# A stored order in place of a list scheduler for the pieces of a banded-attention and MLP kernel

## The chip, the core and the metric

The kernel runs on one core of one Trainium2 chip. The metric is the device time of one launch in microseconds (us); the median of three runs of the kernel before is 668.6 us (666.87 to 668.98).

## The reference

Inputs are q, k, v with batch 4, 8 heads, 768 positions and head size 64, and an MLP with matrices of 512 x 2048 and 2048 x 512. What is computed:

```python
scores = scale * np.matmul(q, k.transpose(0, 1, 3, 2))
is_sink = pos[None, :] < int(n_sink)          # n_sink = 4
rel = pos[:, None] - pos[None, :]
in_window = (rel >= 0) & (rel < int(window))  # window = 128
scores = np.where(is_sink | in_window, scores, -1000000000.0)
a = np.exp(scores - np.max(scores, axis=-1, keepdims=True))
a = a / (np.sum(a, axis=-1, keepdims=True) + 1e-09)
attn = np.matmul(a, v)
x = attn.transpose(0, 2, 1, 3).reshape(B * S, H * D)   # 3072 x 512
h = x @ w_in
out = (h - np.tanh(h)) @ w_out
```

Everything is fp32, and the output is 3072 x 512.

## The kernel before, in words

**Tiling.** The function `_banded` cuts the 3072 tokens into 12 chunks of 256 (a batch and a third of its positions). Each chunk has four attention units u, a pair of heads each, so u runs from 0 to 47. The MLP is done chunk by chunk over 8 groups g of the hidden width, 96 steps n = (chunk, g).

**An attention unit.** Keys come by a DMA at L361, queries by two at L105 (the first twelve units; later L370), into a tile `qk`, `kraw` or `qraw`. Two score pieces on PE (L532 for the first twelve units, L539 after) make `s` and `o`: four matmuls each. DVE merges them with the masks (L554, L556), ACT takes the exponent (L564), DVE the sums and reciprocals (L584, L585), ACT scales (L590; POOL does it for every fourth of the first units, L594), POOL places the sink weights (L601). Then `turn` transposes the probabilities on PE (L624), ACT copies the whole (L631) and DVE two masked parts (L638). For two pairs at a time `attend` multiplies: the sink rows (PE L665, copied by ACT L672 to `zr`), the values (PE L681, L687, with v from the DMAs of L405), and the high and low words of the result (ACT L704, DVE L708) into `xall`, the MLP's input. The sinks' own values come by a DMA at L460, are made high and low words by ACT L466 and POOL L471, and are totalled by DVE L475.

**The MLP.** The raw weights come in halves by SP's queue (L416), DVE decodes them in three passes (L157, L159, L161), ACT and DVE make high and low words (L747, L751), and SP writes what is needed again to DRAM (L755, L761, L762, L765), from where it comes back through a ring of seven slots (L808). The first products (L823) are pieces of six matmuls; then tanh on ACT (L854), the difference on DVE (L857), high and low words (L860 and others; for the chunks from 5 on L873 and, low, L876 into `glbuf`). The second products are L905, or L939, where seven products of blocks stand for eight. Output goes out by POOL and, at the end, by SP and ACT (L996, L1020).

**What sets the order.** Every piece of work is put into a list with `Work.add`: its engine (a DMA counts with the engine that issues it), how long it takes, a due time, a function that issues its instructions, and what it reads and writes. There are 3002 pieces: PE 1038, ACT 593, DVE 748, POOL 194, SP 429. `Work.order` is a list scheduler: it goes through time, gives the engine that can start first the piece that can start on it, the one with the earliest due time first, and reckons delays from engine to engine (`WAKE`) and a time for a DMA to land. At the end of `_banded` the pieces are issued in the order that it gives. Every engine does its pieces in that order and waits, with all that stand behind, until what the next one needs is done.

**Decode buffers.** `turn` puts the transposed probabilities into one of four places m. The places 2 and 3 are also the buffers in which the weights are decoded (`wm[key] = pts[:, 2 + r]`, read and written under the name `("dw", r)`).

Of the kernel before, what the change touches and what calls it, by code (L numbers as in the profile page):

```python
# [169 lines left out]
class Work:  # L170

    WAKE = {"PE": 250, "ACT": 170, "DVE": 90, "POOL": 100, "SP": 80}

    def __init__(self, slack, pad, late, land):
        self.all, self.wrote, self.read = [], {}, {}
        self.slack, self.pad, self.late, self.land = slack, pad, late, land  # L180

    def add(self, engine, took, due, fn, reads=(), writes=(), lands=0, port=False):
        n = len(self.all)
# [9 lines left out]
        self.all.append((engine, took, due, fn, after - {n}, lands, port))  # L193

    def order(self):
        todo = {}
        for n, (engine, *_) in enumerate(self.all):
            todo.setdefault(engine, []).append(n)
        users, left = [[] for _ in self.all], [len(t[4]) for t in self.all]
        for n, t in enumerate(self.all):  # L200
            for a in t[4]:
                users[a].append(n)
        ready = {n: 0.0 for n, k in enumerate(left) if k == 0}
        waiting = {e: [n for n in v if n in ready] for e, v in todo.items()}
        free, port, start, done = dict.fromkeys(todo, 0.0), {}, {}, {}

        def at(n, e):
            t = max(free[e], ready[n])
            return max(t, port.get("DVE" if e == "POOL" else "POOL", 0.0)) if self.all[n][6] else t

        while any(waiting.values()):
            t, e = min((min(at(n, e) for n in v), e) for e, v in waiting.items() if v)
            n = min((n for n in waiting[e] if at(n, e) <= t), key=lambda n: (self.all[n][2], n))
            _, took, _, _, _, lands, locks = self.all[n]
            took *= self.pad if e in ("ACT", "DVE", "POOL") and self.all[n][2] > self.late else 1.0
            waiting[e].remove(n)
            start[n], free[e], done[n] = t, t + took, t + took
            if lands:
                free[e], done[n] = t + (took if e == "POOL" else lands), t + lands + (1700 if self.all[n][2] < self.late else self.land)
            if locks:  # L220
                port[e] = t + took
            for u in users[n]:
                f = self.all[u][0]
                lag = 0 if f == e else self.WAKE[e]
                if f == "PE":
                    lag += self.slack if self.all[u][2] > self.late else 100
                ready[u] = max(ready.get(u, 0.0), done[n] + lag)
                left[u] -= 1
                if not left[u]:
                    waiting[f].append(u)  # L230
# [1169 lines left out]
```

## Time and profile before

| | |
|---|---|
| median of three runs | 668.6 us (666.87 to 668.98) |
| the profiled execution, its own time | 670.4 us |
| its span in the profile | 668.6 us |
| PE (matmul) busy | 650.5 us, 97% |
| weight loads on PE | 603.3 us, 90% |
| DVE busy | 543.8 us, 81% |
| ACT busy | 396.9 us, 59% |
| POOL busy | 164.2 us, 25% |

The span is the time from the first to the last recorded instruction; 1.8 us of the profiled execution lie outside of it. PE is TensorE's matmuls, DVE is VectorE, ACT ScalarE, POOL GpSimd and SP SyncE, which here issues most of the DMAs. L532 is line 532 of the kernel before. In a line of a timeline stand the start and the length in us, the engine, the line, the operation, its output and inputs, and how many instructions the line stands for; in square brackets, how long the engine was idle before it and what ended that.

### The profile page before, as it was taken

Reading aid. Unit: us, or ns where it says so; the run is one execution under the profiler, and the core shown is the slowest. Engines: PE = TensorE matmul, PEld = TensorE weight load, DVE = VectorE, ACT = ScalarE, POOL = GpSimd, SP = SyncE. Lnnn points to the kernel's source line nnn. Section 1 sums busy time; section 2 is a strip of 40 time slices with the busy share of each in tenths; the row PEclk is TensorE's granted clock in tenths of the full one; section 3 lists DMA queues with packets and bytes.
Section 4 is the critical chain, followed back from the end, with each engine's and each line's share of the span. In section 5 each row is a group of like instructions: output and inputs, shape, how many; then the busy total and the mean of one; then the engine's idle time right before and its main releaser. Section 6 shows DMA issues by size and latency. Waiting matters only on the chain.

```text
span 668.6 us, 14547 instructions
## 1 busy us (share of the span) xinstructions
PE 650.5 (97%) x5099; PEld 603.3 (90%) x5099; DVE 543.8 (81%) x1399; ACT 396.9 (59%) x1024; POOL 164.2 (25%) x331
## 2 busy tenths in 40 slices
PE   6989999999999999999999999999999999999996
PEld 4668899999979899898999999999999999999995
DVE  6889999964999878578798899887899899855654
ACT  5987444345898667567665575676566566523321
POOL 5453100000873232243331212312213212100100
PEclk9899999999999999999999999999999999999999
DMA  5877788884999667899977767767776867656771
GB/s 172 279 254 273 260 268 308 292 289 143 226 212 279 217 205 226 236 291 279 287 221 219 223 208 239 251 185 209 243 221 203 266 182 209 206 165 210 259 199 40
DMA packets 79502, 152.97 MB, mean 229 GB/s; under 512 B 9596, under 2 KB 25852, under 8 KB 79420
## 3 DMA queue, kind: packets, MB, share of 16 engines
q1 hardware_dynamic: 65900, 121.52, 58.3%
q0 software_dynamic: 13376, 30.30, 16.1%
q8 instruction: 42, 0.69, 0.4%
q14 instruction: 40, 0.33, 0.1%
q10 hardware_dynamic: 144, 0.13, 0.1%
HBM read 131.47 MB, written 20.45 MB: 227 GB/s over the span
## 4 chain that ended last, share of the span: by engine, by line
PE 76%; DVE 8%; ACT 6%; DMA 4%; issue 2%; POOL 2%; SPq 0%; POOLq 0%; DVEq 0%; ACTq 0%
PE h L823 33%; PE s L939 10%; PE o L939 7%; PE o L905 6%; PE x L687 3%; PE s L905 3%; PE t L624 2%; PE t L687 2%; DMA kraw<-kp 2%; PE t L539 2%; PE t L905 2%; PE x L905 2%; PE x L539 1%; ACT p L590 1%; DVE pt L638 1%
## 5 line engine op out<-in xcount | busy, mean ns | idle before, releaser
L823 PE MATMUL h<-xall,ring 128*128 128x256 f32 x990 | 130.3, 279 | 0.0
L823 PEld LDWEIGHTS h<-xall,ring 128*128 128x128 f32 x990 | 121.1, 188 | 1.4 <-issue 0.7
L854 ACT ACTIVATE gbuf<-h 128x512 f32<-128x512 f32 x96 | 57.1, 595 | 91.4 <-PE h L823 67.6
L823 PE MATMUL h<-xall,spare 128*128 128x256 f32 x738 | 97.6, 279 | 0.0
L873 ACT CAST ghbuf<-gbuf 128x896 fp32r<-128x896 f32 x55 | 51.7, 940 | 68.5 <-DVE gbuf L870 68.4
L823 PEld LDWEIGHTS h<-xall,spare 128*128 128x128 f32 x738 | 90.9, 188 | 0.5
L370 POOL DMA_DIRECT2D qraw<-qd x36 | 26.6, 740 | 255.8 <-DVE q L511 199.9
L876 DVE TENSOR_TENSOR glbuf<-gbuf,ghbuf 128x896 fp32r<-128x896 f32 x55 | 60.0, 1090 | 20.4 <-ACT ghbuf L873 17.5
L564 ACT ACTIVATE p<-p,st 128x132 f32<-128x132 f32 x132 | 52.4, 399 | 12.9 <-DVE st L556 12.0
L857 DVE TENSOR_TENSOR gbuf<-h,gbuf 128x512 f32<-128x512 f32 x55 | 37.9, 689 | 22.9 <-ACT gbuf L854 22.4
L905 PE MATMUL o<-w,ghbuf 128*128 128x512 f32 x192 | 49.9, 395 | 0.2 <-ACT ghbuf L860 0.2
L823 PEld LDWEIGHTS h<-xall,w 128*128 128x128 f32 x384 | 46.9, 188 | 2.0 <-DVE w L751 0.4
L823 PE MATMUL h<-xall,w 128*128 128x256 f32 x384 | 48.2, 279 | 0.2 <-DVE w L751 0.2
L502 DVE TENSOR_TENSOR ks<-kraw,ks 64x392 fp32r<-64x392 f32 x72 | 40.4, 561 | 5.9 <-ACT ks L497 3.8
L590 ACT ACTIVATE p<-p,st 128x132 f32<-128x132 f32 x132 | 42.6, 395 | 3.1 <-DVE st L585 2.6
L905 PEld LDWEIGHTS o<-w,ghbuf 128*128 128x128 f32 x192 | 33.8, 188 | 6.1 <-ACT ghbuf L860 0.5
L857 DVE TENSOR_TENSOR h<-h,gbuf 128x512 f32<-128x512 f32 x41 | 28.5, 696 | 13.0 <-ACT gbuf L854 12.7
L497 ACT CAST ks<-kraw 64x392 fp32r<-64x392 f32 x72 | 37.1, 515 | 2.2 <-DMA kraw<-kp 1.3
L860 ACT CAST ghbuf<-h 128x512 fp32r<-128x512 f32 x41 | 24.0, 585 | 21.1 <-DVE h L857 20.4
L939 PE MATMUL s<-edge,ghbuf 128*128 128x256 f32 x220 | 35.3, 279 | 0.0
L939 PE MATMUL o<-w,ghbuf 128*128 128x256 f32 x220 | 35.1, 278 | 0.0
L939 PE MATMUL s<-w,ghbuf 128*128 128x256 f32 x220 | 35.1, 278 | 0.0
(185 smaller groups left out, 1546.5 us busy)
## 6 DMA issues: line engine op xcount, KB each, us to landing
ring<-wscr SPq DMA_DIRECT2D x165, 256.0 KB, 4.8
spare<-wscr SPq DMA_DIRECT2D x123, 256.0 KB, 4.7
qraw<-qd POOLq DMA_DIRECT2D x36, 256.0 KB, 5.2
...
```

Of the source, the lines that this page charges most:

```text
L497: nc.scalar.copy(ks[u][r, h, :], kt[u][r, :])
L502: (nc.gpsimd if KP else nc.vector).tensor_tensor(k[o, h, :], t[r, :], k[r, h, :].bitcast(F32), op=ALU.subtract)
L564: nc.scalar.activation(e, e, AF.Exp, bias=st[u][:, j : j + 1], scale=-1.0, accum_out=st[u][:, 4 + j : 5 + j],)
L590: nc.scalar.activation(pr[u][:, j, :], pr[u][:, j, :], AF.Copy, scale=s[:, 8 + j : 9 + j])
L687: nc.tensor.matmul(xps[key][(p - p0) // 2][h * 64 : h * 64 + 64, p % 2, a:z], lhsT=vt[cc, i][:, hd : hd + D], rhs=rhs, start=False, stop=p ...
L823: nc.tensor.matmul(hps[n][:, f, :], lhsT=w, rhs=x, start=r == 0, stop=r == 11)
L854: nc.scalar.activation(g0, h(), AF.Tanh)
L857: nc.vector.tensor_tensor(g0 if strassen(n) else h(), h(), g0, op=ALU.subtract)
L873: nc.scalar.copy(ghbuf[:, n % 2], gbuf[:, 1:, :])
L876: nc.vector.tensor_tensor(low7(n), gbuf[:, 1:, :], ghbuf[:, n % 2].bitcast(F32), op=ALU.subtract)
L905: nc.tensor.matmul(sums_of(n, cc, t), lhsT=a[:, f, t * P : (t + 1) * P], rhs=wt[1, g][:, (0, 1, 0)[i], f, :], start=first and not low and ...
L939: nc.tensor.matmul(acc, lhsT=a[:, b, :], rhs=factor(g, m, part % 2), start=g == 0 and part == 0 and m in (4, 1, 2, 7), stop=closes(n) and ...
```

## The change

The scheduler's loop is taken out, and `Work.order` unpacks a table: a permutation of the 3002 pieces, held as text. It asserts that each piece stands behind those that it depends on. The delays, allowances and the due times' use go with the scheduler. `turn` also names the decode buffers among what its copies for the places 2 and 3 read. The offset of the low words in `glbuf` is 4 for the steps 81, 84, 87, 90 and 93, where it was 4 or 44 for 81, 83, 86, 89 and 92.

```diff
-    WAKE = {"PE": 250, "ACT": 170, "DVE": 90, "POOL": 100, "SP": 80}
-
-    def __init__(self, slack, pad, late, land):
+    ORDER = (
+        "c-jruV*?mA69C}k?vhI`wQbwBZQHhO+qP|Et8KemyVb^4uJ8LBo==ZfN{v;ZCMctv3JO&uMJlQqr{=5iDu$Y<teT{}TBH^zR+H62"
...
+    )
+
+    def __init__(self):
         self.all, self.wrote, self.read = [], {}, {}
-        self.slack, self.pad, self.late, self.land = slack, pad, late, land
...
     def order(self):
-        todo = {}
...
-        while any(waiting.values()):
-            t, e = min((min(at(n, e) for n in v), e) for e, v in waiting.items() if v)
-            n = min((n for n in waiting[e] if at(n, e) <= t), key=lambda n: (self.all[n][2], n))
...
-        return sorted(start, key=lambda n: (start[n], n)), start
+        from base64 import b85decode
+        from struct import iter_unpack
+        from zlib import decompress
+
+        todo = [n for n, in iter_unpack("<H", decompress(b85decode(self.ORDER)))]
+        at = {n: i for i, n in enumerate(todo)}
+        assert len(at) == len(todo) == len(self.all)
+        assert all(at[a] < at[n] for n in todo for a in self.all[n][4])
+        return todo
...
-        work = Work(SLK, PAD, LATE, LAND)
+        work = Work()
...
-        ASIDE = {81: 4, 83: 44, 86: 4, 89: 44, 92: 4}
+        ASIDE = {n: 4 for n in (81, 84, 87, 90, 93)}
...
             if c == 0:
-                work.add("ACT", 260, d + 1400, whole, ["t"], [("pt whole", m)])
-            work.add("DVE", 430 if c == 0 else 710, d + 1500, lambda: part(1, below), ["t"], [("pt own", m)])
+                work.add("ACT", 260, d + 1400, whole, ["t"], [("pt whole", m)] + [("dw", m - 2)] * (m > 1))
+            free = [("dw", m - 2)] * (m > 1)
+            work.add("DVE", 430 if c == 0 else 710, d + 1500, lambda: part(1, below), ["t"], [("pt own", m)] + free)
...
-                work.add("DVE", 430 if c == 0 else 710, d + 1500, lambda: part(0, after), ["t"], [("pt before", m)])
+                work.add("DVE", 430 if c == 0 else 710, d + 1500, lambda: part(0, after), ["t"], [("pt before", m)] + free)
...
-        todo, _ = work.order()
+        todo = work.order()
```

Decoded and set beside the list that the scheduler gives, the table has the same 3002 pieces. Of PE's 1038 pieces 405 stand at another place in PE's own list, of ACT's 448, of DVE's 602, of POOL's 165 and of SP's 264. Among themselves, the 864 pieces of the MLP's products stand as before but for four. The beginnings of PE's two lists (scores of unit u are "u2 first" and "u2 second"):

```
place   before             after
 0-3    u0, u1 scores      u0, u1 scores
 4      u2 first           transposes u0
 5      u2 second          u2 first
 6      transposes u0      u2 second
 7, 8   u3 scores          u3 scores
 9      u4 first           sink rows, pairs 0-1
10      transposes u1      u4 first
11      sink rows          transposes u1
12      u4 second          u4 second
13      transposes u2      u5 first
14      u5 first           u5 second
15      values, pairs 0-1  transposes u2
16      u5 second          values, pairs 0-1
```

The beginnings of SP's (each name is the DMAs of that piece; "sinks" are the sinks' values, "w half" is half a raw weight group):

```
place   before             after
 0, 1   u2 keys, queries   u2 keys, queries
 2      v of chunk 0       u3 keys
 3      u3 keys            u4 keys
 4      u3 queries         u3 queries
 5      sinks              u4 queries
 6      w half             w half
 7      u4 keys            sinks
 8      u4 queries         u5 keys
 9      w half             u5 queries
10      u5 keys            v of chunk 0
```

On ACT the copy of u0's transposes stands at place 6 (before: 10), u1's scale at 7 (9), and the sinks' high words at 12 (7). On DVE, u0's two copies stand ahead of u2's merges. The first step's MLP products begin at place 38 of PE's list (before: 40). Further on, SP's writes of decoded weights to DRAM stand up to 27 places earlier, and the v loads of chunk 3 at place 82 instead of 46.

## Rows read from the trace of the kernel before

**Rows 1.** The page, busy time of each engine and share of the span.

```profile
PE 650.5 (97%) x5099; PEld 603.3 (90%) x5099; DVE 543.8 (81%) x1399; ACT 396.9 (59%) x1024; POOL 164.2 (25%) x331
```

**Rows 2.** Waits of PE, 7 to 75 us: releaser, us in total, times, longest.

```profile
PE s L532 <- DVE nswi L556: 2.3, 1, 2.3
PE x L681 <- ACT zr L672: 0.9, 1, 0.9
PE s L532 <- DMA qk<-qd: 0.8, 1, 0.8
PE t L624 <- ACT pt L631: 0.6, 1, 0.6
PE o L532 <- DVE nswi L556: 0.6, 1, 0.6
PE x L665 <- DVE xall L708: 0.5, 1, 0.5
PE h L823 <- DVE w L751: 0.2, 1, 0.2
```

**Rows 3.** Waits of PE, 75 to 669 us.

```profile
PE x L681 <- ACT zr L672: 0.7, 1, 0.7
PE t L624 <- ACT p L590: 0.3, 1, 0.3
PE o L905 <- ACT ghbuf L860: 0.2, 1, 0.2
PE t L539 <- DVE pt L638: 0.2, 1, 0.2
```

**Rows 4.** Windows: PE, PEld, DVE, ACT, POOL busy (count), then clock, DMA share, GB/s.

```profile
15.30:18.00 2.70, 0.40 (x3) 0.04 (x1) 1.06 (x6) 2.63 (x11) 1.27 (x3) 0.98 0.97 327
18.00:21.30 3.30, 3.30 (x11) 2.81 (x12) 1.94 (x10) 3.02 (x14) 0.63 (x3) 0.50 0.42 141
...
75.00:134.00 59.00, 59.00 (x390) 53.78 (x389) 56.21 (x64) 25.34 (x36) 0.00 (x0) 1.00 0.82 288
```

**Rows 5.** Timeline of PE, 12 to 50 us.

```profile
12.29 0.60 PE L624 MATMUL t<-ident,p 128*128 128x128 f32 x4
13.70 1.12 PE L532 MATMUL s<-qk 128*128 128x260 f32 x4 [0.81 <-DMA qk<-qd]
14.65 1.04 PE L532 MATMUL o<-qk 128*128 128x260 f32 x4
17.99 2.07 PE L532 MATMUL s<-qk 128*128 128x260 f32 x4 [2.30 <-DVE nswi L556]
...
49.15 1.77 PE L823 MATMUL h<-xall,w 128*128 128x256 f32 x12
```

**Rows 6.** Timeline of DVE, the end of the merge that the wait is put down to.

```profile
15.07 0.08 DVE L556 DVE_READ_ACCUMULATOR2_ANT nswi<- 128x1 f32 x1
```

**Rows 7.** Timeline of SP's queue: DMA issues, 8 to 13 us.

```profile
8.40 1.05 SPq L405 DMA_DIRECT2D v<-vp  x2
...
11.19 0.67 SPq L460 DMA_DIRECT2D vraw<-vs  x1
11.90 0.44 SPq L416 DMA_DIRECT2D wraw<-w_in  x1
12.38 0.66 SPq L361 DMA_DIRECT2D qk<-kp  x1
```

**Rows 8.** Timeline of ACT, 10 to 18 us.

```profile
10.71 1.29 ACT L590 ACTIVATE p<-p,st 128x132 f32<-128x132 f32 x4
...
15.32 0.62 ACT L466 CAST vsink<-vraw 64x128 fp32r<-64x128 f32 x2 [1.76 <-DMA vraw<-vs]
...
17.93 0.35 ACT L631 COPY pt<-t 128x256 f32<-128x256 f32 x1
```

**Rows 9.** The low words into `glbuf`: ns min/median/max, first and last start.

```profile
L876 DVE TENSOR_TENSOR glbuf<-gbuf,ghbuf x55: 1080/1092/1145, 322.4 to 655.3; 128x896 fp32r<-128x896 f32 x55
```

**Rows 10.** Waits of SP's queue, 0 to 140 us.

```profile
SPq L761 <- DVE pt L161: 35.6, 7, 7.1
```

More of the change, by code (lines that the diff above doesn't have):

```diff
@@ L170 @@
 class Work:
-    WAKE = {"PE": 250, "ACT": 170, "DVE": 90, "POOL": 100, "SP": 80}
-    def __init__(self, slack, pad, late, land):
+    ORDER = (
+        "c-jruV*?mA69C}k?vhI`wQbwBZQHhO+qP|Et8KemyVb^4uJ8LBo==ZfN{v;ZCMctv3JO&uMJlQqr{=5iDu$Y<teT{}TBH^zR+H62"
+        "HA5{{qGqbuDydqcW~ohTikhP$sI6+LnyZ$nh-#kNtoEyIYKuyumaE^?c9l#WP_fnTYK=OmuBt<7hgzYosT*pQnyMnJ!)lt^ss2zm"
+        "RWubvJyt7KJT+adRqNDhbwuq}(bb>ox>~RPQoGbGl};U1kJN3oSH)8M)CQGY?NN8sF||>}RB==abxM6y7u9L?w@R;0sJrSPbyCGu"
+        "XVfS4S^cYytF!8hdZJRQ`0A;;r!FX^AE+Gap}M3{KT}#KQ1=z+uj;uXeOblP=akVe)p?ajeN#DAT>V<b*H_dVW%YLzL#NcQ)LWH7"
+        "rBVqr>lf;sil<ZQgzAUNsNSpcI*m@OeyW7}gK|2LE~rxL|5QZ%OL?7EN79jXew|JS9YH73qNC{OI<-oyhwJn@s?MYeshE1aF0C@?"
+        "GHQg*t7GXZs(?<a^XaN;q)wu<spPt#E~%sGj5@PQq08t}x`HmNC+K9lv`(Wk>DW4(&a6l2a=MVtq9*F>I)|R5E9%iYi>{;#>#RDb"
+        "9;0)qvAU=(qI0Y1x|p7<bLkm+oX)C>>&kkj&aQInS-PGop=;>+s*0YXYwEOWwyveC>E^1s&ZDa8+Ip%ktn#WgdYZ1I*Xp`@oi3u*"
+        ">p41~nycsOqAI`Ipj)UFdZR9>im8=)lP;?|s#SWkUafcN;%bX7p?2!6x|HgqcIk3zo9?A{>)vXQF0T&hA*!0%t1GDO`mnC9_UR+K"
+        "hT5->>WZqiI;Icky6U*DqYmm5x`7(1e$zeRq;9ARsB`+1{$1Bp=XHHuOI^?x^(Ea%UDl`d72Q&u(N}e2)k@vc*Ys_DR<~An^j&>j"
+        "-_z|?6Lmx1*OgQo^*}$=?NnRULH(uw(3RCq9TET5omER63IEhjbSM2(cTs)xBmGQ2*Im^M-Bk5aFLeX`SijS+bYIm?wbJi(XWbLJ"
+        "s}K64{-j^)&$^#_qyN!w^&s`H9;SZiX6lO`uKKH=y00Fg{?oto9aQjDYxt(;>wya3yB?_qD1^bv0f7Mz4fO(TL7;~kr2_O+5r82g"
+        "G}85SB!~=+bqt6CQ6VO@*3lpqG||x^HjGwnbR1}|o9VdFR>y<*&{QXZ1kge!grtxNl0iG298y3Roe~m5D(I?HLk4KCGeS3=3Hs^G"
+        "&`WpMS)jijqtZZD=%BMfS{R_SLpsO<IUqgs)On$Y?yWoOe2^3J!$MsEa=}2oNEd`ckQ)laVqF3T=_R@(6oFE(RF{S_P!yKwvanni"
+        "gCV*c6o<Q59`0ck=mQm?FI0t!FcPXkC8!RAbq%Nt{a~oB3ALa$G=PTC2pU5ZXaRMgDYS&T&<grPJ!l54p*{?N=FkD!KtCJ^gRmov"
+        "fMGaHcY@B)1ujE37=?piFkFHDcoo`0FSrKnU?_~k_HY{pV`Q8JQ(!XOfeA1buERu_19xEv41;?x7w*Gw7>+k!8a#kea1%!3bQlc}"
+        "VLZ-+TQCFufLSmG#=<g~hkwHgSPql$Pnd=);R!5(S@;Mxz-(BAOW`Rj!)GuLR^dh%2hU+XjEDL70v^LEn2ZB(HN1pZumF0)TKEgr"
+        ";cIvgn{Wuef$6vlw&4d@1M6THj=+zw2X@0k*a3Ut6TF3;@EH!l7<>oo;U72*`(P6c#D8Hk?1wM#6BfZ1*oR+XF+{-wa1gq}H|P%k"
+        "!311@zd=&`1;2yBp_mM}LUPoY5|2P8Oo874Fclt!*@(Ce2s7e#I0mWl2Y5__i}5&|g5@Z90#3sjI0>sU9j3*R7%)8=JPYe_3g*Pk"
+        "I0NTkZrqMbFc0R%TzC#vpv7Vs0rMeaemoBuuqejGvA7#AKxUkX@o)`Zge<rpqvBL7fYI<i7Q}4m@C6panHU}CVp%MVG4Lgx!T1;x"
+        "Utt0)kFoFpCd6_W8z16ptbi4<7XE=n@Ec~wOYkSg!S9$DpWs6Lfse2fZotQw6`$f?xD;z*W!!=*@fq&GvseY6;~UI@Z}D&ZiNE1H"
+        "ERI4Yuo?!cj_<J{mc)NB0)4=>*a-i{#@G%^VO4B`U+^O~#jjWc|HEdu5r1J@{DcvyG%EUx@u(3s$J)3R>!7Ci)B-Ifpq6+9%V1q>"
+        "g(ncGH8TB<ZO{=?J#0bk(GyX9j6@x<0Y;{T)Cu=sI_ikcC<<M`&UgT$QcFrt&8aKKq72jxJ5wu)P0^?|9mVcws12ROwiJirQakEI"
+        "?WqeUqUh8EGg1tSNjtG8_M%>R4m(gEN=*GI3GKyv)R&S{f67n2DHRo<WYm#{Q*ug8hj17j!vU0n22vX8jcF+pb)l5hl?GEm8bX;V"
+        "3w5J%)Cb2=BFswVX*}hk3Y3jz(*(**lV~Dkr#v*7x>F9yOFd{1&7vuE5vNii8cKz!A|1plScFDUPufo-sVE(wBsiTK(?Oa+rKkx_"
+        "qtUd4a#CsPi;L(m&ZMPOhQ?4?I)#^TELEanw3wDrW%`YZ(|WprRp=re#}afEms3@`M02PXm88p5jYiR2s!l6t9o44OxRUD7DymDX"
+        "sRpf~->DuopqqGzuFzUKOpj?EZJ_z|7agIEw17_1-?We#m`zlZPSG{oOs8oJZKE@EmYULbx=KfBEA60b^n@Cj`m~c8n`6|_9H(2@"
+        ")-*A@=p5~)^LU+3&>p%$P0eL&WA4&kx=FXFnYl;JO$&3MTAJI`$~>Tl^e=s(F6JverPijac}CypJl&z^6iheM&b*-RCW5(+Zz-aA"
+        "Nj=OvYHxa)_cXwCG=I<s>SVstZ5(Jin;#U(e56;@!ThAe<~8*)Nlb6^AN4V4lA1U4i~5=iL`IoWrk~Nq7;D({H<8T<Gsr|S$;=ot"
+        "(nK|bO?ETdOf}IAm>g!P$!VgS*k+jdlZKl(W~>=!rkL?2uK7gq%mkC%#4tn5MDvJZnp`G@iEk#El%}+qY*LvrW|~QF%9_+BmYHYL"
+        "m<(pRnQt<h1!kt1VKSM_W|sL(xs5Zk%^Z`*lrw3~LX+1dFmp{llg_L#i%fpA*c3J^%@VVZikJeXpebsWnq{V#DQ@<feP+KYZ<d>y"
+        "wt_ieR+);XkU3{on@Z*%I&apR%4UtJZq}LlHjCL{)|(n;qiJ9_nJT8H@n*BBZN${I4Jo0yU>e#)W{at3x0*(_mZ@sCnU?mTX=Q&i"
+        "+f6ld(fn>6np(ELIb`aZKg@CSr#Wm+n4PAvJz}z&lctG1Wlo!>_KZ1dn%PUHx$SI^nak#p>0+;#7WRWVYp$A(_M^FFy4p_mleuPY"
+        "n>(hp?Psr>yQYo3XG)lE_P)7c9-DTyt-WbJo4-tZ+t>bW9{iu{iLthWt!-Z#wolC~Q^&kE&&)3K#ymG~O?Ugw^sq0?Kc=Ml*St5*"
+        "_O!ih9GlI2F~e;g`_;s?z3qP{p8aNi8D;y}QbyYmcBlpW-Jtchza3@=Sh4Z#4-;&9JJS9%5$q_N!49$$ZAMErs*Pr&+rf6Ajc8-o"
+        "AvUI+WMkP#Hi3<7N83y`p{-}e*eEuUEo8^q*mj&PY!lnrcDzkti`XPKrA=ig*f}<}ooUn9$u_A?Yp2-EHkr+0=h~unmQ8N6+HH28"
+        "U1qb{-DbN@XQ$a6Hn*K>r`zl{kIidm*c~RH&0+J~`8KC5V3*orc7e@hi`$)cp)Fwx+T(VSJz*EylC~0;vnOpSyT_EbOKfRd!B(=%"
+        "ZADwguCTjoWxLx};Zt^{tzygCJ@%GeWpCTPwuW76f3tUNRlCmqZr9sGcD1d>hwVPQ#vZXp?S6aOR^|=%u03Gub5%ZQt8+cxXgAq2"
+        "cC$Tex7e5VoIPe=*&6)X*5u3fyuD(t+6(rYt<4whb=!h(*j8MJ@7YWCzI|hB@lE@{{%7m*L)(&n*=F3D|FVi3@E`VX`@}ZqhWyn2"
+        "X*=^X``kXVowzZ-wN1DYKeq2|Q`Y?6zOYfb4M*d){K5Wfqw`1m#eTKz_>*nV9r&B=!{2R3{$W2`;9iW}mt*ihwl@=};C|eN4X5O;"
+        "+@FPi+F_iE19#`)9DyzO;D}t!_T)$$nVARhK#s|SI2Na7$AdXH$L1mIIS%LHp&W%1a$Ziv6F4!C;JBQGM{-h*$H_Q8r{PJQmd9~E"
+        "PQdASJg?@7oStX%8cxnxcrB0S$((_+ayA~r-8egE<Q!bx=H#)QpJ#C<p2F*R6c^yBoS6&qR=ba<aV{?IrgI_Q&oj6<AK=1Vf@g9O"
+        "F3EGa6c^>Wyq@QCS$B}<@dhr<<=sXu!{@oQTfmEW6JOwBypVt6#e9*=@)G`?FY$K%gDdh<F5@<HIaiLC@fNP&wsLj1gIDlQuHkm^"
+        "a^A+fc_r`RLtN4Q$(7t;uI%>m34X*?+!3zoPVy;k<W6%nca+cYS+40W^D(aFuJB`S?CQ7%?jv92<6O@*bl3P3H*x2<t-H;2-DkeT"
+        "ce%d1&Q0AtZsyv!=I%bP;ufx@yTK3mCjZ5Mb1U}`-{L21U2FG{pEA3y?iD-N-M!{+?hQZVcJ3_?ay{L1e#h<Id+y=><rn;gz3b&("
+        "az_`}4Rl|*vn$~~@HdX<esLF9+r@X^`TzZOo!k#D>A>}NeH^+DuAlqK<iwS7|8a2rT>{tFMQ|CMabsLWm(dMy(Of1M$whaAT?{wG"
+        "MRqY=EH~E0c2QhHH_T;riQI5E%8hV|-3k}gjdn@gN;l3;cX3=wx5}k*<vFz*>5{rMZoEtDlDTPaf~&w2T{@TCWpP8@WVhO-a8q1X"
+        "m(5LbyIp#h-R*HxT^_gB<#01xUN_U_bopE^m){lhv)pXA#?5g>{9HHR758i1K3Blaa|_%$SJW?bXIyT#-W7Cb-6FT#mGFh!Iakar"
+        "c7@#rx6y5JOWjtt#BFoiT}i*gEprw8PPfUG@<rT!SJ9XDo819--j(qO-7a_EmGuu?IscnG>K?k^-7$CEmG>uHEq~Hg@`v0hSJ_{1"
+        "hh0@)!~fwfx@!K2yX0#7cdm{<?Jm3b?uPr|>iR40rn}{8`X>IiyXu<yJFdFF>;81tTs{BM)%TCwb@$kzZ{Y8_hMxRiu90u&pF89K"
+        "b}w9e|I&5vPh4aF%Dr|^T^s+#eR3WBGxymw^VYZZ&HX<vmVfJd`hQ()-@~``ar_te!&UKL-B0(QYvq4A<y(90zqwAHeP{pOIUm<|"
+        "@m)RmwBGvxUi=`R&JXmFeK()p2S3(F@lkzuU(`kOgMD-#!4L5<d@mo*NA$gYe4oJ&^$C0=Ki7}(ef>P&!YB0od@?`Z_xH(t3Ln!C"
+        "^C|sspU9{3sr?9_(I@sJeG<RGXY!+bW}nn=@LBvupHtHKg+8}z@_8hu&+0e(ypqdj^P_!kpHK4myndW7D%t&bzsUFTi+w)-yU*b#"
+        "`UyV2KjfGAmHx0_<qP;Jezh;?r}{~Lji2VX_{qMopYD(NrGA;uB{Td?Urd(!wSJag=U4cxezxD{ulV(TyT9u5%Qe5l7mz)Euixi)"
+        "`a-hb@ABp4fG;ZteMKoONBwSp%wPBAq@W!4fBWBj5jo+X__MyaJoOdioG&5geI>czYf33O=`Z?Pa><|aH+)Gs?Qi;LzO>x(XZ#mG"
+        "$Cr`Y{;R+2ANX&+vQ&{f{-OWFSCv2gU0+Qe`RdY89{a}f+~4yx<c0t4Ys*W2-v?<TuY4nkAWh{jUq{~ii1NXI^v&e8uP1foldmtI"
+        "eOvj*H;^B`oxJhQ<*kn-h5S$dpKl@Wd?NYf6U)DzB#E>VC9TDXm6pPy#YuPZ(nfknWC7_aQ6#DKl=c!;P{vCyi6$Lnf{4VHi4sS;"
+        "NhgUeaiyblmUt3F;!6VQBFQAC^p;7IT>3~XNg<0Qp`?_>(odF1D(NrjB)w#k43b(hN*b9gnI)}Ek)@JF`pQ(<D$`_uY?G`qTeeF!"
+        "$su!OuFR8xGF|4&0vRMTWSPvAA+kf3%V3!$E997Dm*KKdR?2Z%Cnsd6tdjMzK~~E~*(Aecv#gPwvP(|NTG=f(WsB^QTXIlt%U=0S"
+        "ewTf6NDj+>IU=XzfSi^)a#YU93ppz<<&wOTb8=a($Ot(vSLK3Slk0L<F3LT5EhFWI+?Sv7K>m}*@=G4dU-Gy7Ay4E_c`DE3jf@f%"
+        "M$034E^p<XL<#RDYWPQ@g%9$te37y8QNGG2`6k~*hcWV5AVd#81VfrYA#Ly>T`)mH2sT6r<0N8;6gb2PF@p=~L#&WLL=Le-fsh~+"
+        "3~@rj5H}<Vi9*tlIK&GXLh6t)Bn$CFp^zz53aLWoP&woXRYLNRCFBe#LavZC<PIrAo{%l%4TVGYP$X0h`9jgqG!zTXLg~;v6c1%W"
+        "*-#>s3nfGOP$5(cr9$=4B2)}DLXS{0^bGYvuTU%04-G=?&@j{qjY8wlGSm&NLhsNdv<{;~n=mGH3}Zvv&?$5d?LwE(K6DM;LZ8qf"
+        "^bO-e_s}oQ3;o0VFeEGp1H#ZSEDQ|8!=NxCj11$$;4mR945PxtFeywAlf#TKGfWAy!qhN3%n6Iaw6HkL4NJn(uqrGItHbiJF02Xb"
+        "!-}vrtPGpNhOjwo2^+)Kur2He+rzG~Gwcbw!`|>eHRAmL"
+    )
@@ L195, in order @@
     def order(self):
-        todo = {}
[L197 to L209, printed above, removed]
-        while any(waiting.values()):
-            t, e = min((min(at(n, e) for n in v), e) for e, v in waiting.items() if v)
-            n = min((n for n in waiting[e] if at(n, e) <= t), key=lambda n: (self.all[n][2], n))
[L214 to L230, printed above, removed]
-        return sorted(start, key=lambda n: (start[n], n)), start
+        from base64 import b85decode
[6 more added lines that the diff above has]
+        return todo
 def _banded(tc, qd, kp, vp, vs, small, masks, w_in, w_out, ident, pts, early, out):
```

## The prediction, made before the change was run

> **What bounds the kernel now.** I read the page's busy times first: PE is busy for 650.5 of 668.6 us [rows 1]. The change adds and removes no instruction, so PE's work stays as it is and all that an order can give lies in the 18.1 us in which PE is not busy, and in stretches in which it is busy but slow. The second view is PE's waits, cut at 75 us. From 7 to 75 us it lists seven, 5.9 us in all [rows 2]; from 75 us to the end four, 1.4 us in all [rows 3]. The rest, some 11 us, is the start ahead of the first scores, the end behind the last matmul and gaps that no wait is put down to; the table leaves the start's and the end's work where it is, so I count no gain there. The third view is the table of windows. From 15.3 to 18 us PE is busy for 0.40 of 2.70 us while the DMA engines are busy for 97%; from 18 to 21.3 us PE is busy throughout, but at a granted clock of 0.50, that is at 1.2 instead of 2.4 GHz [rows 4]. It is the price of the hole before it: the first scores of u4 took 2.07 us there, where those of u3 took 1.04 to 1.12 [rows 5]. With the transposes and sink rows of that stretch, 3.30 us at half the clock are 1.7 us lost. So the sum at stake is 5.9 + 1.7 + 1.4 = 9.0 us.
>
> **The longest wait is not what its label says.** The first scores of u4 waited 2.30 us, put down to DVE's merge [rows 2, 5]. That merge had ended at 15.15 us [rows 6], nearly three before 17.99. What was late is the load of u4's keys: SP issued it at 12.38 us, behind the v of chunk 0 (1.05 us of issue), the sinks' values (0.67) and half a weight group (0.44) [rows 7]. At the same time ACT stood 1.76 us for the sinks' values, with u1's scale and the copy of u0's transposes behind it; that copy ran at 17.93 us, though the transposes had been there since 12.9 [rows 5, 8].
>
> **The change part by part, the loads.** In the table u3's and u4's keys and queries stand in front of the v, the sinks and the weight half. u4's loads are then issued about 2.2 us earlier (1.05 + 0.67 + 0.44), and fewer bytes stand ahead of them; counted from 17.99 they are there by 15.8 at the latest. The v of chunk 0 goes out some 7 us later, by the issue times of what now stands ahead of it, and is wanted by the values, the 17th piece of PE's list; weights are decoded later still. I cost both at nothing; if the v were the late one, it would take back what u4 gained, 1.5 us.
>
> **PE's list to u4.** Transposes of u0 now stand ahead of u2's scores. They need u0's scale, which ends at 12.00 [rows 8], so they stay at 12.29, and PE is idle for some 2.1 us from the end of u1's scores. u2's two pieces follow (12.7 and 13.65), at the 0.95 us from one piece to the next that rows 5 show between 13.70 and 14.65; then u3's (14.6 and 15.5), then short sink rows, then u4's first at some 16.5. The loads no longer decide. That is 1.5 us ahead of 17.99, and the first big hole is now ahead of 12.29, smaller by 0.2 than the one it replaces and filled behind with three units' scores in a row. ACT does the copy of u0 at once, then u1's scale, and the sinks' high words come five places later, by when they have landed; so ACT's 1.76 us [rows 8] go. The copies on DVE stand ahead of u2's merges, which wait for u2's scores anyhow.
>
> **The clock.** With PE fed from 12.3 us on I take the 1.7 us of slow clock as not coming back. Both ends: 0 gained (it falls somewhere else) and 1.7. I take 1.7, since the row at 0.50 follows a stretch with 0.40 us of work in 2.70 [rows 4], and no such stretch is left behind 12.3 us. Together, the 17th piece of PE's list ends 1.5 + 1.7 = 3.2 us ahead.
>
> **From there to 75 us** the list of waits still holds 0.9 + 0.6 + 0.6 + 0.5 + 0.2 = 2.8 us [rows 2]. Going down the four lists piece by piece with the durations of the trace, the first MLP product starts 5.5 us ahead of its 49.15 [rows 5], with 1.4 us of transposes and scores now behind it instead of before it, so 4.1 in truth; with the values of chunk 2, a set of pieces that is complete in both orders, it is 4.7. So 1.5 of the 2.8 go. This walk counts no time for a handover from engine to engine; about 25 of them lie on the way. From the end of u0's scale, 12.00, to its transposes, 12.29 [rows 5, 8], it is 0.29 us, but PE still had other work then, so that is the upper end, and nothing the lower; I take 0.05, near the lower, since most handovers lie under work of the waiting engine: 1.3 us off. **3.2 + 1.5 − 1.3 = 3.4 us** early on. Ends: nothing, and the 7.6 us of waits and slow clock.
>
> **After 75 us** PE is busy for 59.00 of 59 us up to 134 and waits 1.4 us in all afterwards [rows 3, 4]. The table shifts the attention pieces by up to ten places among the products, and takes away the 0.7 us for `zr` and the 0.3 for `p` by putting the waiting pieces some places later. It also leaves less PE work than before ahead of some transposes and second scores (units 19, 20, 27, 36), by 0.1 to 0.4 us each, 0.9 in all, and where that cover is what hid the chain of DVE and ACT, a new wait is up to as long. 1.4 − 0.9 = 0.5, of which I keep **0.3**. Ends: −0.9 and +1.4.
>
> **What costs nothing.** The four product pieces that stand otherwise are moved among pieces of the same step or the next. The offset in `glbuf` moves where low words are written: over 55 of them at all offsets the time runs from 1080 to 1145 ns [rows 9], DVE is not the bound there, and the ends are 0 and 5 x 0.07 us. The extra names in `turn` add no semaphore; they only bind the order. POOL's sinks of u0 and u1 stand ahead of three memsets for units that come tens of us later. Output stores go out later by some places, but the last ones stay last.
>
> **The sum:** 3.4 + 0.3 = 3.7 us. The profiled execution took 670.4 (span 668.6), so 666.7 against it; it lies 1.8 above the median of the runs, 668.6, so **664.9 us** by the median.
>
> **Rivals.** *The gain is lost before 134 us.* From 75 to 134 us DVE is busy for 56.21 of 59 us, 95% [rows 4], decoding weights for products that PE does at once. If DVE is the true bound there, PE arriving 3.4 us early only finds weights not decoded: up to 3.4 us of new waits for `w`. For it: the 95%, and that decoding stands later in DVE's list than before in the early phase. Against: DVE's own holes before 49 us are in part the ones that close, so it comes early too. It would give 668.6 less 0 to 0.5, about 668.3.
>
> *SP is held up by its own spills, and the kernel is slower.* SP's writes of decoded words wait for DVE, 35.6 us in seven waits, up to 7.1 [rows 10], and what stands behind them in SP's list waits too. The table puts other writes up to 27 places forward, and one weight half of group 4 now stands behind such a wait where it stood before. It decides if a half is then issued with less than its landing ahead of its decoding; I count at least 8 us ahead. A hold of the longest kind, 7.1, leaves 0.9 of them; u4's keys took up to 5.6 us to land (12.38 to 17.99), so the decoding is 4.7 us late, PE, busy throughout until then, waits that long, and the slow clock behind the hole costs the 1.7 of rows 4 again: 6.4 − 3.7 = 2.7 us slower, 671.3.
>
> *The clock falls elsewhere.* The new hole of 2.1 us ahead of 12.29 can bring the slow clock by itself, as the one at 15.3 did [rows 4]. Then u2's and u3's scores run at half the pace and 1.7 of the gain is gone: 2.0 us, 666.6. The Trainium skill (TensorE: Matmul & The Clock Gate, What's actually happening) says that throttled is the default state and that activity releases it, so by that rule an idle stretch is paid for wherever it stands, and the sum would be the 666.6 of this rival; rows 4 agree in that the 0.50 came behind the hole.
>
> *The table says little.* Some 1880 of 3002 pieces stand elsewhere, but most by a few places inside work that PE's dense stream hides; if u4 turns out to wait for something that is not on SP's queue, nothing is left: 668.6.
>
> **How the numbers follow.** About 0.3% (2.0 us) is what a measurement of this kernel can tell from no change; faster is below 666.6, slower above 670.6. The forecast has 0.55 (0.50 of it faster, 0.05 same), the gain lost before 134 us 0.20 (0.02 faster, 0.15 same, 0.03 slower), SP's hold 0.11 (slower), the clock 0.10 (0.06 faster, 0.04 same, being on the border), little 0.04 (same). Faster 0.58, same 0.28, slower 0.14. The range runs from 661.0, which has 7.6 of the 9.0 us gained, to 669.8, past both cases without gain; SP's hold and a complete gain are left out, some 0.15 together.
>
> **What would show it.** Right: u4's first scores at 16 to 17 us with no wait over 0.5; no stretch at a clock of 0.50 behind 15 us; the first MLP product at 43.5 to 45 us; waits of PE from 7 to 75 us at about 2.1 us for u0's transposes and under 1.5 for the rest; after 75 us under 2 us in all. Wrong: waits of `h` for DVE's `w` between 60 and 134 us (the first rival), the same with SP's L416 issued late behind L755 or L761 (the second), a clock of 0.50 between 10 and 16 us (the third), u4 still at 18 us (the fourth).

## The result: slower, by 9 us

The changed kernel takes 677.86 us (median of four runs, 675.71 to 681.92), the kernel before beside it 668.79: a ratio of 1.0145, with a 95% interval of 1.0122 to 1.0167. The profiled execution took 677.01 us, with a span of 675.2. PE's work is the same 5099 matmuls, but PE's busy time has grown by 4.6 us over [rows 1]:

```profile
PE 655.1 (97%) x5099; PEld 605.9 (90%) x5099; DVE 547.9 (81%) x1399; ACT 396.9 (59%) x1024; POOL 156.4 (23%) x331
```

PE's waits in the changed kernel, first from 7 to 75 us, then from 75 us on (releaser, us in total, times, longest):

```profile
PE s L567 <- DVE st L591: 3.7, 1, 3.7
PE t L659 <- ACT pt L666: 1.1, 1, 1.1
PE t L659 <- DVE pt L673: 1.0, 1, 1.0
PE x L701 <- DVE xall L744: 0.7, 1, 0.7
...
PE s L941 <- ACT ghbuf L896: 1.4, 1, 1.4
PE h L859 <- DVE w L787: 0.8, 1, 0.8
PE s L975 <- ACT ghbuf L909: 0.8, 1, 0.8
PE t L659 <- ACT p L625: 0.2, 1, 0.2
```

The 2.3 us of u4's scores [rows 2] are gone as forecast (in e7 too, where nothing holds up the start). In their place the largest wait is one of u1's scores, 3.7 us, which was not there at all; and from 75 us on the list grows from 1.4 [rows 3] to 3.2 us. The windows show what follows the first (PE, PEld, DVE, ACT, POOL busy, granted clock, DMA share, GB/s):

```profile
7.60:15.30 7.70, 4.00 (x11) 2.72 (x9) 4.38 (x23) 3.01 (x13) 1.14 (x3) 0.72 0.65 191
15.30:18.00 2.70, 2.59 (x10) 1.86 (x9) 1.69 (x9) 2.53 (x11) 0.63 (x3) 0.53 0.84 280
18.00:21.30 3.30, 3.30 (x18) 2.85 (x17) 2.95 (x19) 3.30 (x17) 1.09 (x4) 1.00 0.95 315
...
75.00:134.00 59.00, 58.16 (x381) 52.44 (x380) 51.62 (x59) 22.78 (x35) 0.00 (x0) 1.00 0.80 287
```

The stretch at half the clock has moved from 18 to 21.3 us [rows 4] to one that ends before 18, behind the new hole; and from 75 to 134 us DVE does 4.6 us less than it did (51.62 against 56.21 [rows 4]).

Waits do not say where the time went, since small ones are not listed. So for each piece on PE I took the time from its start to the next piece's start, in this profile less in that of before, and added it up by when the piece ran before. This gives us lost (+) or gained (−) by stretch; three of the experiments below stand beside it:

```
stretch (us, before)   0-62  62-128  128-140  140-300  300-400  400-600  600-end    sum
changed kernel        -0.57   -0.30    +3.13    +0.98    -0.68    +4.11    -0.14   +6.53
memset back (e2)      -3.21   -0.31    +3.29    +3.96    -0.53    +4.04    -0.14   +7.10
and loads (e5)        -4.71   -0.32     0.00    +2.49    -0.57    +4.11    -0.14   +0.86
three undone (e7)     -4.93   -0.32     0.00    +0.03    -0.39    +0.41    -0.73   -5.93
```

The changed kernel's sum agrees with the start of the last piece, 667.91 against 661.40. Each row is one profiled execution, so its scatter is in it: e2 and e5 have the same order up to 62 us and differ there by 1.5 us. There are three places: the start, where a gain is eaten up; 128 to 140 us; and everything behind 140, where no single wait is large.

**The start.** Ahead of `_banded`, DVE makes the masks. One of its instructions there, at L136, compares four columns with the window (`nc.vector.tensor_scalar(near, near, window, None, op0=ALU.is_lt)`). DVE's and POOL's timelines, changed kernel:

```profile
4.76 4.00 DVE L136 TENSOR_SCALAR pt<-pt,nswi 128x4 f32<-128x4 f32 x1
...
4.75 0.21 POOL L479 IOTA nswi<- 128x2 int32 x2 [1.50 <-issue]
4.90 0.32 POOL L480 MEMSET vsink<- 128x256 f32 x1
5.15 0.32 POOL L481 MEMSET z<- 128x256 f32 x1
5.40 0.54 POOL L412 MEMSET qraw<- 128x512 f32 x1
5.87 2.87 POOL L412 MEMSET qk<- 128x512 f32 x6
```

and the same of the kernel before:

```profile
4.76 0.51 DVE L136 TENSOR_SCALAR pt<-pt,nswi 128x4 f32<-128x4 f32 x1
...
4.72 0.53 POOL L377 MEMSET qraw<- 128x512 f32 x1 [1.47 <-issue]
5.19 0.21 POOL L444 IOTA nswi<- 128x2 int32 x2
5.34 0.32 POOL L445 MEMSET vsink<- 128x256 f32 x1
5.58 0.32 POOL L446 MEMSET z<- 128x256 f32 x1
5.84 4.27 POOL L377 MEMSET qk<- 128x512 f32 x9
```

The instruction takes 0.22 us when no memset stands beside it (e2 below). In the changed kernel it took 4.00 us and ended (8.76) when POOL's last memset ended (8.74). In the kernel before it was held too, but by one memset only: it ended at 5.27, the first memset at 5.25, and what followed on POOL was an IOTA, though POOL went on without a gap to 10.11. Behind it on DVE stand two small mask instructions and the read of the value on which the kernel branches (L80), so u0's first merge began at 11.57 instead of 7.72, and u1's scores, which need its score tile free, at 11.93 instead of 8.11. The table had put the sinks' start, two memsets with an IOTA ahead of them, in front of the query tile's memset.

**128 to 140 us.** DVE's waits, 49 to 140 us, the first line of each: the changed kernel, then before.

```profile
DVE pt L157 <- DMA bscr<-pt: 4.6, 2, 2.7
```

```profile
DVE h L857 <- ACT gbuf L854: 3.2, 5, 1.2
```

L157 is the first pass of decoding; its buffer is free only when the decoded words before have been written to DRAM. The timelines of DVE and PE in the changed kernel:

```profile
114.82 0.69 DVE L157 TENSOR_SCALAR pt<-wraw 128x1024 uint32<-128x1024 uint32 x1 [1.88 <-DMA bscr<-pt]
...
128.46 0.69 DVE L157 TENSOR_SCALAR pt<-wraw 128x1024 uint32<-128x1024 uint32 x1 [2.73 <-DMA bscr<-pt]
...
132.07 0.50 PE L859 MATMUL h<-xh,w 128*128 128x256 f32 x2 [0.83 <-DVE w L787]
...
136.30 2.11 PE L941 MATMUL s<-w,ghbuf 128*128 128x512 f32 x8 [1.44 <-ACT ghbuf L896]
```

What the second of these waited for are two DMAs, here in the changed kernel and then before, with the pass that took the buffer without a wait:

```profile
119.72 0.33 SPq L797 DMA_DIRECT2D bscr<-pt  x1
120.88 0.32 SPq L798 DMA_DIRECT2D bscr<-pt  x1
```

```profile
114.97 0.32 SPq L761 DMA_DIRECT2D bscr<-pt  x1
115.33 0.43 SPq L762 DMA_DIRECT2D bscr<-pt  x1
...
122.08 0.69 DVE L157 TENSOR_SCALAR pt<-wraw 128x1024 uint32<-128x1024 uint32 x1
```

In the changed kernel the first was issued right behind the decoding (the last pass ended at 119.64); the second came 0.8 us later than it might have, as SP waited for another DMA. From the second issue the buffer was free 7.6 us later (128.46); before, it was taken 6.75 us after it. The DMA engines were busy throughout when the writes were issued (421 and 413 GB/s from 118 to 120 and from 120 to 122 us); before, they were nearly idle (39 GB/s from 114 to 116 us).

### The profile page after: what moved, and what is told of

The parts are those of the page before. It is cut to its first block, busy times and chain, and to the rows that moved or that the text cites. A ratio compares the mean times of both kernels' runs of the same rounds, so it can differ in the third digit from the quotient of the medians.

```text
span 675.2 us, 14510 instructions
## 1 busy us (share of the span) xinstructions
PE 655.1 (97%) x5099; PEld 605.9 (90%) x5099; DVE 547.9 (81%) x1399; ACT 396.9 (59%) x1024; POOL 156.4 (23%) x331
## 3 DMA queue, kind: packets, MB, share of 16 engines
q0 software_dynamic: 13376, 30.30, 16.5%
## 4 chain that ended last, share of the span: by engine, by line
PE 83%; DVE 7%; DMA 5%; ACT 2%; issue 1%; DVEq 0%; POOL 0%; SPq 0%; ACTq 0%; POOLq 0%
PE h L859 34%; PE s L975 10%; PE o L941 10%; PE o L975 8%; PE x L723 4%; PE t L659 3%; PE t L723 2%; DMA wraw<-w_out 2%; PE t L574 2%; PE s L574 2%; PE x L574 2%; PE s L941 2%; PE s L567 1%; DMA bscr<-pt 1%; DMA wraw<-w_in 1%
## 5 line engine op out<-in xcount | busy, mean ns | idle before, releaser
L396 POOL DMA_DIRECT2D kraw<-kp x36 | 22.1, 613 | 105.4 <-DVE ks L537 72.1
L673 DVE TENSOR_TENSOR pt<-t,below 128x512 f32<-128x512 f32 (+1 forms) x48 | 28.7, 598 | 9.0 <-PE t L659 6.7
```

## The experiments

All of them change the stored order alone. The edits stand behind the decoding of the table; `old` is the scheduler's order, stored in the same way. Where `old` is used, the extra names in `turn`, which issue nothing, are left out.

**Is it the order? e1.**

```diff
+        todo = old
```

> All else as in the changed kernel (a stored table, the new offsets of the low words), but the table holds the scheduler's order. Theory 1 (the time lies in the order alone): as the kernel before, 668 to 669.5 us, with the wait of 2.3 us ahead of u4's scores. Rival (the offsets, or the way in which the order is stored, cost the time): 672 us or more.

Measured: 668.87 us, ratio 0.9993 (0.998 to 1.0006). The offsets of the low words and the storing cost nothing that can be told from scatter; what follows is the order.

**The start: e2, e4, e12.** First the memset put back in the table (piece 2 is the query tile's memset, 0 the sinks' start):

```diff
+        todo.remove(2)
+        todo.insert(todo.index(0), 2)
```

> The new order, but on POOL the first memset of a query tile stands ahead of the sinks' start again, as before. Theory 1 (DVE's four-element mask instruction at L136 is held up by POOL's unbroken run of memsets, and that is what u1's scores waited for): L136 takes about 0.5 us instead of 4.0, u1's first scores start by 8.5 us instead of 11.93, and the whole is about 3.5 to 4 us faster than the new order, 674 us. Rival (the start's loss is hidden by what is late behind it): L136 is short, but the time stays within 1 us of 677.9.

Measured: 675.48 us, ratio 1.009 (1.0071 to 1.0108), 2.4 below the changed kernel. L136 took 0.22 us, u1's first scores began at 8.47, no stretch behind 7.6 us had less than the full clock. DVE's instruction, and POOL's first memset:

```profile
4.76 0.22 DVE L136 TENSOR_SCALAR pt<-pt,nswi 128x4 f32<-128x4 f32 x1
...
4.93 0.53 POOL L414 MEMSET qraw<- 128x512 f32 x1 [1.68 <-issue]
```

The mechanism is as expected and the gain smaller than the 3.5 to 4 us: 2.4 by the medians, 3.0 if each kernel is set against the one before that was measured beside it (9.1 less 6.1). The profiled execution of e2 was the slowest of its six (677.65; the others 673.53 to 675.71), so its row of the table does not stand for the median. In e5's row the start is worth 4.1 us up to 62 us (−4.71 against −0.57), and 1.5 of them are lost again from 140 to 300 (2.49 against 0.98). That the pieces there reach PE earlier, but not what they wait for, is argued from these rows and not tested. Then the exchange alone, in the scheduler's order:

```diff
+        todo = old
+        todo.remove(0)
+        todo.insert(todo.index(2), 0)
```

> The scheduler's order with one exchange: on POOL the sinks' start ahead of the first memset of a query tile. Theory 1: L136 on DVE takes 3.5 us or more longer (the memsets run on to some 10 us), u0's first merge starts at 11 us or later, and the time is 3 to 5 us above the kernel before, 672 to 674 us. Rival (it takes the other moves too): L136 stays at 0.5 us and the time within 1 us of the kernel before.

Measured: 668.41 us by the median, ratio 1.0011 (0.9987 to 1.0035), and yet not the rival. The twelve runs fall into two groups, seven from 667.05 to 668.44 and five from 672.49 to 673.93. The profiled one is of the second (673.57), and has the hold of the whole run of memsets, longer here since nine follow instead of six:

```profile
4.76 5.39 DVE L136 TENSOR_SCALAR pt<-pt,nswi 128x4 f32<-128x4 f32 x1
```

So the hold comes in some runs only; the medians of the two groups lie 5.6 us apart. That the seven faster runs had no hold is inferred, since none of them was profiled. Small shifts in time seem to decide: in e2 the first memset starts at 4.93 and does not hold L136, in e4 it starts at 4.89, behind two IOTAs, and does. The last of the three shortens the run, with the exchange still in place:

```diff
+        todo = old
+        todo.remove(0)
+        todo.insert(todo.index(2), 0)
+        late = [11, 14, 17, 20, 23, 26, 29]
+        at = todo.index(150) + 1
+        todo = [n for n in todo[:at] if n not in late] + late + todo[at:]
```

> The scheduler's order with the sinks' start ahead of the first memset of a query tile, as in the exchange alone, and seven of the memsets that followed (units 5 to 11) put behind the sinks of u0, so that POOL's unbroken run ends at some 7 us instead of 10. Theory 1 (the instruction at L136 is held for as long as the run lasts): L136 takes 2.3 us at most where POOL came first, the runs no longer fall into two groups 5 us apart, and the time is within 1.5 us of the kernel before. Rival (the exchange itself delays L136, whatever follows): 5 us of L136 in some runs, and two groups again.

Measured: 669.33 us, ratio 0.9997 (0.9986 to 1.0009), twelve runs from 668.02 to 670.61 in one group. POOL's last memset of the run ends at 6.87 us, L136 at 6.90:

```profile
4.77 2.13 DVE L136 TENSOR_SCALAR pt<-pt,nswi 128x4 f32<-128x4 f32 x1
...
5.87 1.00 POOL L486 MEMSET qk<- 128x512 f32 x2
```

Three lengths of the run, three lengths of the instruction: 2.13, 4.00 and 5.39 us, for 5, 9 and 12 memsets behind one another. That is the cause of the first loss. How long the hold is does not by itself say what it costs: with the 2.13 us of e12 the time is that of the kernel before. In the changed kernel one execution of four was profiled, so how often the hold comes there is not known; its runs spread over 6.2 us.

**The new start without the rest: e3.**

```diff
+        todo.remove(2)
+        todo.insert(todo.index(0), 2)
+        head = todo[:279]
+        todo = head + [n for n in old if n not in set(head)]
```

> The table's first 279 pieces (PE's first 58, up to some 62 us of the changed kernel) with the memset back, then all others as the scheduler had them. Theory 1 (the new start is good but for the memsets, and the loss behind 130 us is the table's later part): the lead of some 4.5 us at 62 us is kept, 664 to 665.5 us, no wait of PE for a decoded weight. Rival (DVE's decoding or the loads bound the stretch up to 134 us, so a lead can't be kept): 668 to 669 us, with waits of PE between 62 and 134 us.

Measured: 667.29 us, ratio 0.9974 (0.9962 to 0.9986). A miss in size: by pieces 4.6 us are gained up to 62 us, as expected, but 1.95 are lost again from 62 to 100, at the seam of the two orders. A cut elsewhere was needed to see the lead by itself (e7).

**The late writes: e5, e8.** In SP's list of the table, three loads of the weight ring and the three of chunk 3's v stand ahead of these writes; before they came later, but for the v, which was long done. At 256 KB each they are 1.5 MB, some 5.5 us by an estimate at the 287 GB/s of the window from 75 to 134 us. e5 and e8 move all of them together; which of them makes the writes late is not told apart. e5 puts them behind:

```diff
+        todo.remove(2)
+        todo.insert(todo.index(0), 2)
+        at = todo.index(356) + 1
+        late = [781, 782, 986, 346]
+        todo = [n for n in todo[:at] if n not in late] + late + todo[at:]
```

> The new order with the memset back, and on SP four loads (three of the weight ring for steps 24 and 25, and the v of chunk 3) put behind the writes of group 5's decoded words to DRAM. Theory 2 (those loads fill the DMA engines ahead of the writes, the writes land late, DVE's next decoding waits 4.7 us for its buffer, and PE for the weight and the gate): DVE's waits for those writes fall under 1 us, PE's waits from 75 to 150 us (2.3) go, and the time is 2.5 to 3.3 us below the 675.5 of the order with the memset back, 672.5 us. Rival (DVE is 95% busy there and late by itself): the waits stay, over 674.5 us.

Measured: 672.09 us, ratio 1.0042 (1.0023 to 1.006), 3.4 below e2. DVE's list of waits no longer has the writes, and its first line is now

```profile
DVE glbuf L904 <- ACT ghbuf L901: 1.3, 2, 0.7
```

and PE loses 0.00 us from 128 to 140. e8 turns it round: the table with the memset back up to 136 us, the loads where the table has them, then the scheduler's order.

```diff
+        todo.remove(2)
+        todo.insert(todo.index(0), 2)
+        head = todo[:552]
+        todo = head + [n for n in old if n not in set(head)]
```

> As the one with three losses undone, but with the four loads where the table has them: the early lead and the late writes, without the table's later part. Theory 2: the 3.3 us that PE loses from 128 to 140 us are in it and eat up the lead, 669 us, so the later part alone makes up the 6 us between it and the order with the memset back. Rival: 666 us, the writes cost nothing without what follows.

Measured: 668.62 us, ratio 0.9982 (0.9972 to 0.9992), with the waits for the writes back (4.7 us) and 4.5 us of PE lost from 128 to 140. That DVE is busy for 95% is not what bounds this stretch: with the loads behind, DVE keeps up with a PE that is 5 us earlier (in e7 below PE is busy for 59.00 of 59 us from 75 to 134, DVE for 56.34).

**All three undone: e7.** The edit of e5, and then

```diff
+        head = todo[:552]
+        todo = head + [n for n in old if n not in set(head)]
```

> The table's first 552 pieces (to 136 us) with the memset back and the four loads behind the writes, then the scheduler's order. Theory (the three losses are all there is): only the early lead of 3.2 to 3.5 us is left, 666 us. Rival (the lead is lost again at the seam or behind it, as 2 of 4.6 us were where the seam stood at 62 us): 667.5 us or more.

Measured: 664.19 us (663.78 to 664.76), ratio 0.9916 (0.9901 to 0.9931). It beats both kernels: 5.4 us below the one before. PE's waits from 7 to 75 us, and, from PE's timeline, the first product:

```profile
PE t L734 <- ACT pt L741: 1.1, 1, 1.1
PE t L734 <- DVE pt L748: 0.9, 1, 0.9
PE t L734 <- ACT p L700: 0.9, 2, 0.6
PE x L775 <- DVE xall L818: 0.7, 1, 0.7
```

```profile
43.66 2.33 PE L933 MATMUL h<-xall,w 128*128 128x256 f32 x18
```

5.9 us of waits [rows 2] have become 3.6, no clock is lost, and the first product starts 5.5 us earlier than at 49.15 [rows 5]. By the medians, from the kernel before (669.62 beside e7) to the changed one: the lead −5.4, the table behind 136 us +7.9 (e5 less e7), the late writes +3.4 (e2 less e5), the start +2.4 (the changed kernel less e2), 8.2 in all. These steps make a chain, so that they add up shows nothing. What tests them is the writes, which were priced twice: +3.4 with the table behind them and +4.4 with the scheduler's order (e8 less e7). Prices of one step differ by some 1 us with what else is in the kernel.

**The table's later part: e6, e10, e9, e11.** e6 takes the scheduler's order up to 353 us and the table from there:

```diff
+        head = old[:1608]
+        todo = head + [n for n in todo if n not in set(head)]
```

> The scheduler's first 1608 pieces (to 353 us of the kernel before), then all others in the table's order, with the new kernel's offsets. Theory 3 (the attention's pieces stand too close behind what they need in the table's later part): 3.5 to 4.5 us of it come here, so 673 to 674 us against 669.4, in many steps of 0.1 to 0.5 us. Rival (the later loss is only carried on from the start: pieces shifted against transfers that are late): within 1 us of the kernel before.

Measured: 673.25 us, ratio 1.006 (1.0038 to 1.0082). By pieces 4.0 us are lost from 400 to 600, as in the changed kernel (4.1): this part is made there, not carried there. It is 3.6 us of the 7.9 behind 136 us; the rest, made between 136 and 353 us, no run takes apart. e10 was meant as e6 with SP's list left as the scheduler had it; its edit is another table, in which the other engines' pieces stand as in e6 and SP's as in `old`:

> The same kernel with the table's order from 353 us on, but SP's own list there as the scheduler had it. Theory 3 (the loss is one of PE, ACT and DVE): no change, 672.8 to 673.8 us. Rival (SP's loads and stores stand late in the table, as they did at 100 to 130 us): 670 us.

Measured: 674.09 us (672.69 to 674.97), ratio 1.0078 (1.0055 to 1.0101), by pieces 4.4 us from 400 to 600. But its edit changes nothing: behind the scheduler's first 1608 pieces, those of SP that are left stand in the table in the scheduler's order, so e6 has the scheduler's SP list already, and e10 is e6 again in the order of every engine. What it shows is scatter. The rival falls by e6 itself, which has the loss with the scheduler's SP list. So it is the order of PE, ACT, DVE and POOL, POOL's loads included; these were not told apart. One unit's transposes in the changed kernel show the kind of step (PE's timeline):

```profile
508.57 0.27 PE L659 MATMUL t<-ident,p 128*128 128x128 f32 x1
509.06 0.63 PE L659 MATMUL t<-ident,p 128*128 128x128 f32 x3 [0.23 <-ACT p L625]
```

Its unit's scaling on ACT ran from 508.01 to 509.31, behind a cast of the gate's at 506.94; before, PE did the same four in 0.60 us from 504.86, in one go, as ACT had begun at 503.49. From 350 to 600 us, the 54 weight loads of transposes that carry a wait start 154 ns behind the load ahead of them, against 115 before: 2.1 us. I took that for the cause and gave the transposes more cover. e9 is e6 with the transposes of the units 29 to 47 two product pieces later each; e11 is e5 with those of 16 to 47 so. Their edits are tables again, and PE's is the only list that differs.

> The kernel with the table's order from 353 us on alone, with one move: PE's transposes of the units 29 to 47 stand two pieces of the products later each. Theory 3 (too little PE work stands between ACT's scaling of a unit and PE's transposes of it): of the 3.6 us lost behind 350 us the 2.1 that the transposes wait go, 671 to 671.8 us against 673.25. Rival (ACT and DVE are late there whatever PE does, and the copies behind the transposes pass the wait on to the products): 672.8 to 673.8 us.

> The table with the memset back and the four loads behind the writes (672.1 us), and PE's transposes of the units 16 to 47 two pieces of the products later each. Theory 3: the waits of transposes for ACT's scaling go over the whole of the table's later part, 3 to 4 us of the 7.4 that it loses behind 140 us, 668 to 669 us. Rival (only PE's place in the list changes, the waits move to the copies and the gate): 671.5 us or more.

Measured: 684.16 us, ratio 1.0222 (1.0191 to 1.0254), and 692.43, ratio 1.0353 (1.0321 to 1.0386). Both far out, and on the other side. PE's waits in e9, 350 to 600 us:

```profile
PE t L574 <- DVE pt L673: 4.7, 8, 0.8
PE s L974 <- ACT ghbuf L908: 1.4, 2, 1.1
PE t L574 <- ACT pt L666: 0.9, 1, 0.9
...
PE t L574 <- DVE xall L743: 0.5, 1, 0.5
```

The transposes' waits have gone (112 ns from load to load), and the next unit's scores (L574) wait instead: their 36 loads for `t` that carry a wait start 380 ns behind the one ahead, where it was 152 in e6. Transposes and scores share the score tile `t`; the scores of the next unit can't start before DVE has copied the transposes out. A unit goes round in a ring, scores, exponent, scaling, transposes, copies, next scores, and what one place is given is taken from the next. DVE's waits for the transposes in the same stretch, e9 and then e6, show the other half:

```profile
DVE pt L673 <- PE t L659: 10.3, 10, 2.0
```

```profile
DVE pt L743 <- PE t L729: 1.4, 3, 0.8
```

DVE's list was left as it was, so DVE stood at the copies until the later transposes came, with all its other work behind them. So e9 and e11 show that cover on PE alone makes it worse; they do not show what moving the copies along with the transposes would do. In e11 the loss begins at 250 us, so the move costs there as well. Which moves made the table's later part slow is not settled.

## Why the prediction was wrong

I forecast 664.9 us, in a range from 661.0 to 669.8; it is 677.86. The gain early on was there; three steps that were put at nothing or nearly so cost more than it. The largest is "After 75 us", whose cause is in part open.

- **u4's loads, PE's list, the clock: right in the main.** 3.4 us were to be gained early on; with the memset back it is 4.6 to 4.9 up to 62 us (e3, e5, e7, e8), and 3.2 in the one of e2 that was profiled. u4's first scores start at 16.48 us in e7, without a wait, where 16.5 was said, and the slow clock does not come back. The first product starts at 43.66, the 5.5 us ahead that the walk gave; the 1.3 us taken off it for handovers do not show. The parts of the waits came out otherwise than the sum: u0's transposes wait 0.9 us and not 2.1, the rest 2.7 and not under 1.5. That e7's median, 664.19, lies so near to 664.9 is luck: it has the larger lead, and none of the gain counted after 75 us.
- **The step that failed first is "what costs nothing"**, with its sentence on POOL's list, and the one ahead of it that the start's work is left where it is. I looked at which pieces wait for POOL, and not at what runs on DVE beside it. The exchange of the first two pieces on POOL was in the lists; it stands in no step. It cost 2.4 to 3.0 us here, and 5.6 where the run is longer.
- **The second rival had the right place and the wrong handle.** SP's writes of decoded words do hold up the decoding, and PE waits for `w`, as it says. But the writes were issued late by 0.8 us at most, and the weight halves came in time; the writes landed late behind other loads, and it was the buffer that DVE waited for. 3.4 to 4.4 us, where I priced the case at 6.4 and gave it 0.11. The moves of the ring's loads and of chunk 3's v stand in no step of the prediction: it asks of a load whether it comes in time for itself, and not what is behind it on the DMA engines.
- **"After 75 us" is the step that failed by the most: 0.3 gained, ends −0.9 and +1.4; it is 7.9 lost behind 136 us, beside the late writes.** The units named as short of cover are not where it lies: in the changed kernel units 19, 20 and 36 lose 0.8 us together at their transposes and scores, where 0.9 was reckoned for the four, and unit 27's transposes gain 0.6. From 400 to 600 us the 4.1 us stand in some 30 steps of 0.1 to 0.5 us, 1.8 of them at product pieces, 1.5 at transposes and 0.8 at scores. I summed the cover of PE alone, place by place; e9 shows that it is shared round the ring through ACT and DVE. What in the table's order uses it up stays open; e6 shows that nearly half of the loss is made behind 353 us, and without SP's list.
- **The first rival fell**: DVE's 95% did not eat up the lead. **The third was not put to the test at its size**: the hole of 2.1 us ahead of u0's transposes came out as 0.6 and 0.3 us in e2 and e7, and they brought no slow clock. The slow clock that did come stands behind 3.7 us of idle PE.

The Trainium skill (SBUF — State Buffer, SBUF: two separate sides) says that POOL and some of DVE's instructions share one pair of ports, which goes as an exclusive lock to whichever starts first for the whole of its instruction, the other being blocked. The holds above agree in that DVE stood until a memset of POOL's ended. The measurement differs in two points. The price is not one instruction: where memset followed memset, DVE got nothing between them, up to 5.39 us over 12 of them; where an IOTA stood behind the first memset, DVE was through at that memset's end (0.49 to 0.60 us in nine of the fourteen profiles). And the starts as recorded do not tell who loses: in e3 L136 starts at 4.76, the memset at 4.81, and L136 is held for 0.60 us. One instruction of POOL's, at most 0.54 us here, would have made the exchange a small rival; that the hold lasts 4 to 5 us had to be measured.
